# A second layer with seven products in place of eight, and casts and transposes that take strict turns

## The chip, the cores and the metric

The kernel runs on one core of a Trainium2 chip. The metric is the device time of one execution in microseconds (us). The profile gives the *span*, from the first to the last instruction; a timed execution is some 1.7 to 2.3 us longer than its span (401.6 for a span of 399.7, 428.7 for 426.6). A run is called slow when it is over 1.5% above the fastest of the same kernel, and only fast runs are compared.

## The reference

```python
# x, f_logit: (4, 6144, 256) float32; lower_bound: (256,)
sig = 1 / (1 + exp(-f_logit))
f = lower_bound + (1 - lower_bound) * sig
for t in range(6144):                      # a recurrence along the sequence
    h = f[:, t] * h + (1 - f[:, t]) * x[:, t]
    y[:, t] = h
y = y.reshape(24576, 256)
out = maximum(y @ w1, y @ w2) @ w_out      # w1, w2: (256, 1024); w_out: (1024, 256)
```

## The kernel before

The tokens come in *blocks* of 512, 48 of them, and two blocks make a *chunk* of 1024 (the first four blocks are chunks of their own, so chunks 4 to 25 hold two blocks each: 22 chunks, 21 periods between them). The kernel uses max(a, b) = a + relu(b - a): the *first layer* gives relu(y (w2 - w1)), and the *second layer* adds y (w1 w_out) to relu(...) w_out. So a block needs 16 first-layer products with 512 columns and 40 second-layer products with 256 columns.

The recurrence wants channels on partitions, and the inputs lie the other way round. From chunk 4 on, each input goes through three steps: a *cast* (a DMA on GpSimd's queue, float32 to bf16, into a scratch in memory), a *transpose* (a DMA on SyncE's queue, scratch to the tile fT or xT), and then the *gate* (a sigmoid on ScalarE), decay, drive and scan on VectorE. Each tensor has two scratches. A cast waits only until the transpose that last read its scratch has landed.

```python
    def fetch(c):
        b, t0, nt, _ = chunks[c]
        for s in range(2):
            src = srcs[s][b, t0 : t0 + nt, :]
            if by_xbar(c, s):
                scr = scratch[s][uses[s] % NSCR]
                uses[s] += 1
                nc.gpsimd.dma_start(
                    out=scr[0:nt, :].rearrange("(p i) d -> p (i d)", p=P),
                    in_=src.rearrange("(p i) d -> p (i d)", p=P),
                )
                held[c, s] = scr
            else:
                nat = natpool.tile([P, CH // P, D], BF16, name=("fn", "xn")[s])
                nc.gpsimd.dma_start(
                    out=nat[:, 0 : nt // P, :].rearrange(
                        "p (k i) d -> p k (i d)", i=TB // P
                    ),
                    in_=src.rearrange(
                        "(k p i) d -> p k (i d)", p=P, i=TB // P
                    ),
                )
                held[c, s] = nat
# ... cut ...
    def cross(c):
        nt = chunks[c][2]
        for s in range(2):
            if by_xbar(c, s):
                dst = inpool.tile([P, KC, CH], BF16, name=("fT", "xT")[s])
                nc.sync.dma_start_transpose(
                    out=dst[:, :, 0:nt], in_=held[c, s][0:nt, :]
                )
                held[c, s] = dst
# ... cut ...
    def gate(j):
        nb = blocks[j][2]
        u = midpool.tile([P, KC, TB], BF16, name="u")
        fT = turned[j, 0]
        nc.scalar.activation(
            out=like(u[:, :, 0:nb], fT), in_=fT, func=AF.Sigmoid, scale=-1.0
        )
        us[j] = u
# ... cut ...
    def first_layer(j, fc):
        nb = blocks[j][2]
        y = ys[j]
        dT = ps_d.tile([P, TB], FP32, name="dT")
        for kc in range(KC):
            nc.tensor.matmul(
                dT[:, 0:nb],
                lhsT=wd[:, kc, fc * P : (fc + 1) * P],
                rhs=y[:, kc, 0:nb],
                start=(kc == 0),
                stop=(kc == KC - 1),
            )
        rt = rpool.tile([P, TB], BF16, name="rt")
        nc.scalar.activation(out=rt[:, 0:nb], in_=dT[:, 0:nb], func=AF.Relu)
        rts[j, fc] = rt
# ... cut ...
            left = y[:, s, i:nb:ns] if s < KC else rts[j, s - KC][:, i:nb:ns]
            right = w13[:, s, :] if s < KC else wob[:, s - KC, :]
            nc.tensor.matmul(
                ps[:, r, :],
                lhsT=left,
                rhs=right,
                start=(s == 0 and (r == 0 or j == NBLK - 1)),
                stop=(s == n - 1 and (r == 1 or j == NBLK - 1)),
                skip_group_check=True,
            )
# ... cut ...
    LEAD_FETCH = 7
    LEAD_CROSS = 3
    done = {"fetch": 0, "cross": 0}

    def ahead(kind, fn, j):
        while done[kind] < NCHUNK and chunks[done[kind]][3] <= j:
            fn(done[kind])
            done[kind] += 1
# ... cut ...
        for j in range(2, NBLK + 1):
            ahead("cross", cross, j + LEAD_CROSS)
            ahead("fetch", fetch, j + LEAD_FETCH)
            steps = turn_steps(j + 2) if j + 2 < NBLK else []
            gates = {}
            if j + 1 < NBLK and by_xbar(blocks[j + 1][3], 0):
                gates[0] = j + 1
            if j + 2 < NBLK and not by_xbar(blocks[j + 2][3], 0):
                gates[FC // 2] = j + 2
            # ... cut ...
                if j < NBLK:
                    first_layer(j, fc)
                if j > 2:
                    second_layer(j - 1, fc)
                n = len(steps)
                turn(steps[fc * n // FC : (fc + 1) * n // FC])
                if fc in gates:
                    gate(gates[fc])
                if fc == 0 and 2 < j < NBLK - 1:
                    scans = scan_steps(j + 1)
                if fc < len(scans):
                    scans[fc]()
```

In block j the loop does the gate of block j+1, the scan of block j+1, the first layer of block j and the second layer of block j-1.

Of the kernel before, what the change touches and what calls it, by code (L numbers as in the profile page):

```python
# [18 lines left out]
def kernel(  # L19
# [18 lines left out]
    CH = 1024  # L38
    assert S % CH == 0

# [15 lines left out]
    def by_xbar(c, s):  # L56
        return c >= 4
# [6 lines left out]
    natpool = ctx.enter_context(tc.tile_pool(name="nat", bufs=6))  # L64
    inpool = ctx.enter_context(tc.tile_pool(name="inp", bufs=5))
    midpool = ctx.enter_context(tc.tile_pool(name="mid", bufs=2))
    ypool = ctx.enter_context(tc.tile_pool(name="ypool", bufs=4))
    rpool = ctx.enter_context(tc.tile_pool(name="rpool", bufs=2 * FC + 4))
    opool = ctx.enter_context(tc.tile_pool(name="opool", bufs=4))
    ps_t = ctx.enter_context(  # L70
        tc.tile_pool(name="ps_t", bufs=2, space=bass.MemoryType.PSUM)
    )
    ps_d = ctx.enter_context(
        tc.tile_pool(name="ps_d", bufs=3, space=bass.MemoryType.PSUM)
    )
    ps_o = ctx.enter_context(
        tc.tile_pool(name="ps_o", bufs=3, space=bass.MemoryType.PSUM)
    )

    NSCR = 2  # L80
    scratch = [
        [dram.tile([CH, D], BF16, name=f"scr{s}_{q}") for q in range(NSCR)]
        for s in range(2)
    ]
    uses = [0, 0]
# [5 lines left out]
    def fetch(c):  # L91
        b, t0, nt, _ = chunks[c]
        for s in range(2):
            src = srcs[s][b, t0 : t0 + nt, :]
            if by_xbar(c, s):
                scr = scratch[s][uses[s] % NSCR]
                uses[s] += 1
                nc.gpsimd.dma_start(  # L98
                    out=scr[0:nt, :].rearrange("(p i) d -> p (i d)", p=P),
                    in_=src.rearrange("(p i) d -> p (i d)", p=P),  # L100
                )
                held[c, s] = scr
            else:
                nat = natpool.tile([P, CH // P, D], BF16, name=("fn", "xn")[s])
                nc.gpsimd.dma_start(
                    out=nat[:, 0 : nt // P, :].rearrange(
                        "p (k i) d -> p k (i d)", i=TB // P
                    ),
                    in_=src.rearrange(
                        "(k p i) d -> p k (i d)", p=P, i=TB // P  # L110
                    ),
                )
                held[c, s] = nat
# [3 lines left out]
    def fetch_first(k):  # L117
        nt = TB // 2
        for s in range(2):
            raw = const.tile([P, nt // P, D], FP32, name=f"raw{k}{s}")  # L120
            nc.sync.dma_start(  # L121
                out=raw[:],
                in_=srcs[s][0, k * nt : (k + 1) * nt, :].rearrange(
                    "(p i) d -> p i d", p=P
                ),
            )
            raws[k, s] = raw

    def first_bf16(k, s, copy):
        raw = raws[k, s]  # L130
        nat = const.tile([P, raw.shape[1], D], BF16, name=f"nat{k}{s}")
        copy(out=nat[:], in_=raw[:])
        raws[k, s] = nat

    def first_turn(k):
        nt = TB // 2
        for s in range(2):
            dst = ps_t.tile([P, KC, nt // P, P], BF16, name="tT")
# [9 lines left out]
    def cross(c):  # L148
        nt = chunks[c][2]
        for s in range(2):  # L150
            if by_xbar(c, s):
                dst = inpool.tile([P, KC, CH], BF16, name=("fT", "xT")[s])
                nc.sync.dma_start_transpose(  # L153
                    out=dst[:, :, 0:nt], in_=held[c, s][0:nt, :]
                )
                held[c, s] = dst

    def turn_steps(j):
        b, t0, nb, c, o = blocks[j]
        steps = []  # L160
        for s in range(2):
            if by_xbar(c, s):
                turned[j, s] = held[c, s][:, :, o : o + nb]
                continue
            dst = ps_t.tile([P, KC, TB], BF16, name="tT")
            ns = nb // P
            turned[j, s] = dst[:, :, 0:nb].rearrange("p k (i m) -> p k m i", i=ns)
            for q in range(ns):
                for h in range(KC):
                    steps.append(  # L170
                        (
                            dst[:, h, q * P : (q + 1) * P],
                            held[c, s][:, o // P + q, h * P : (h + 1) * P],
                        )
                    )
# [7 lines left out]

    us = {}

    def gate(j):
        nb = blocks[j][2]
        u = midpool.tile([P, KC, TB], BF16, name="u")
        fT = turned[j, 0]
        nc.scalar.activation(  # L190
            out=like(u[:, :, 0:nb], fT), in_=fT, func=AF.Sigmoid, scale=-1.0
        )
        us[j] = u
# [6 lines left out]
    def scan_steps(j):  # L200
        b, t0, nb, c, o = blocks[j]
        u = us[j]
        ff = midpool.tile([P, KC, TB], BF16, name="ff")
        v = midpool.tile([P, KC, TB], BF16, name="v")
        y = ypool.tile([P, KC, TB], BF16, name="y")
        ys[j] = y

        def decay(h):
            nc.vector.tensor_scalar(  # L209
                out=ff[:, h, 0:nb],  # L210
                in0=u[:, h, 0:nb],
                scalar1=nom[:, h : h + 1],
                scalar2=1.0,
                op0=ALU.mult,
                op1=ALU.add,
            )

        def drive():
            xT = turned[j, 1]
            nc.vector.tensor_tensor(  # L220
                out=like(v[:, :, 0:nb], xT),
                in0=like(u[:, :, 0:nb], xT),
                in1=xT,
                op=ALU.mult,
            )

        def scan(h):
            if t0 == 0:
                init = 0.0
            else:  # L230
                pn = blocks[j - 1][2]
                init = ys[j - 1][:, h, pn - 1 : pn]
            nc.vector.tensor_tensor_scan(  # L233
                out=y[:, h, 0:nb],
                data0=ff[:, h, 0:nb],
                data1=v[:, h, 0:nb],
                initial=init,
                op0=ALU.mult,
                op1=ALU.add,
            )  # L240

        return [
            lambda: decay(0),
            lambda: decay(1),
            drive,
            lambda: scan(0),
            lambda: scan(1),
        ]

    first = {}  # L250

    def first_recurrence(k):
        nt = TB // 2
        cols = slice(k * nt, (k + 1) * nt)
        if k == 0:
            for t in ("u", "ff", "v"):
                first[t] = midpool.tile([P, KC, TB], BF16, name=t)
            ys[0] = ypool.tile([P, KC, TB], BF16, name="y")
        u, ff, v, y = (*(first[t] for t in ("u", "ff", "v")), ys[0])
        fT, xT = raws[k, 0], raws[k, 1]  # L260
        nc.scalar.activation(
            out=like(u[:, :, cols], fT), in_=fT, func=AF.Sigmoid, scale=-1.0
        )
        for h in range(KC):
# [7 lines left out]
            )  # L272
        nc.vector.tensor_tensor(
            out=like(v[:, :, cols], xT), in0=like(u[:, :, cols], xT), in1=xT,
            op=ALU.mult,
        )
        for h in range(KC):
# [13 lines left out]

    ident_f = const.tile([P, P], FP32)
# [8 lines left out]
    wdf = wpool.tile([P, KC, DFF], FP32)  # L301
    wd = wpool.tile([P, KC, DFF], BF16)
    w1T = wpool.tile([P, FC, D], BF16)
    w13 = wpool.tile([P, KC, D], BF16)
    NG = 2
    NQ = FC // NG
    w1n = [wpool.tile([P, KC, NQ * P], FP32, name=f"w1n{g}") for g in range(NG)]
    w2n = [wpool.tile([P, KC, NQ * P], FP32, name=f"w2n{g}") for g in range(NG)]

    def half(w, g):  # L310
        return w[g][:].rearrange("p kc (m q) -> p kc q m", q=NQ)

    def fcs(w, kc, g):
        return w[:, kc, g * NQ * P : (g + 1) * NQ * P].rearrange(
            "p (q m) -> p q m", q=NQ
        )
# [12 lines left out]
    def make_wd(fc, n):  # L329
        g, r = divmod(fc, NQ)  # L330
        qs = slice(r, r + n)
        cols = slice(fc * P, (fc + n) * P)
        nc.vector.tensor_tensor(  # L333
            out=wdf[:, :, cols].rearrange("p kc (q m) -> p kc q m", q=n),
# [4 lines left out]
        for kc in range(KC):  # L339
            if g == 0:  # L340
                nc.scalar.mul(wd[:, kc, cols], wdf[:, kc, cols], om[:, kc : kc + 1])  # L341
            else:
                nc.vector.tensor_scalar_mul(
                    out=wd[:, kc, cols], in0=wdf[:, kc, cols], scalar1=om[:, kc : kc + 1]
                )

    def turn_w1(k):
        g, r = divmod(k, NQ // 2)
        pt = ps_o.tile([P, KC, 2, P], FP32, name="psO")
# [11 lines left out]
    def make_w13():  # L361
        for kc in range(KC):
            psw = ps_o.tile([P, 2, D], FP32, name="psO")
# [9 lines left out]

    rts = {}

    def first_layer(j, fc):
        nb = blocks[j][2]
        y = ys[j]
        dT = ps_d.tile([P, TB], FP32, name="dT")
        for kc in range(KC):  # L380
            nc.tensor.matmul(  # L381
                dT[:, 0:nb],
                lhsT=wd[:, kc, fc * P : (fc + 1) * P],
                rhs=y[:, kc, 0:nb],
# [3 lines left out]
        rt = rpool.tile([P, TB], BF16, name="rt")  # L388
        nc.scalar.activation(out=rt[:, 0:nb], in_=dT[:, 0:nb], func=AF.Relu)  # L389
        rts[j, fc] = rt  # L390
# [3 lines left out]
    def second_layer(j, slot):  # L394
        b, t0, nb, c, o = blocks[j]
        ns = nb // P
# [3 lines left out]
        for k in range(slot * total // FC, (slot + 1) * total // FC):  # L400
            i, s = divmod(k, n)
            g, r = divmod(i, 2)
            if s == 0 and (r == 0 or j == NBLK - 1):
                acc["ps"] = ps_o.tile([P, 2, D], FP32, name="psO")
# [3 lines left out]
            left = y[:, s, i:nb:ns] if s < KC else rts[j, s - KC][:, i:nb:ns]  # L408
            right = w13[:, s, :] if s < KC else wob[:, s - KC, :]
# [8 lines left out]
            if j == NBLK - 1 and s == n - 1:  # L418
# [3 lines left out]
                r0 = b * S + t0  # L422
                (nc.sync if r else nc.scalar).dma_start(
# [148 lines left out]
```

## Time and profile before

The three runs took 438.17, 401.23 and 438.83 us. It has a fast and a slow state. The profile is of the slow one.

| | kernel before, slow profile |
|---|---|
| span | 428.3 us |
| TensorE / ScalarE / VectorE busy | 92% / 63% / 58% |
| transposes, issue to landing (medians) | 15 to 16 us for fT, 9 for xT |
| chunk period (issue of transposes to the next) | 11 to 23 us, mean 17.0 |

The page of the kernel before gives the span, the chain of work that ended last (share of the span by engine, then by line) and, per group, busy time, mean ns of one, then idle time before the group and what ended it:

```profile
span 428.3 us, 6970 instructions
...
PE 46%; DMA 34%; SPq 15%; ACT 3%; DVE 1%; issue 1%; ACTq 0%
PE psO L410 25%; DMA fT<-scr_0_90 20%; PE dT L381 19%; SPq L153 13%; DMA fT<-scr_1_91 12%; ACT u L190 2%; DMA w1n_110<-in_moe_w_dram 2%; SPq L433 1%; PE psO L352 1%; ACT rt L389 1%; PE tT L180 1%; PE psO L365 0%; SPq L121 0%; DVE osb L430 0%; DVE y L233 0%
...
L389 ACT ACTIVATE rt<-dT 128x512 bf16<-128x512 f32 x384 | 219.2, 598 | 104.1 <-PE dT L381 100.0
L381 PE MATMUL dT<-y,wd 128*128 128x512 bf16 x720 | 219.5, 384 | 21.3 <-ACT rt L389 19.5
L410 PE MATMUL psO<-wob,rt 128*128 128x256 bf16 x1536 | 230.7, 274 | 2.7 <-issue 0.4
...
L190 ACT ACTIVATE u<-fT 128x1024 bf16<-128x1024 bf16 x44 | 46.4, 1054 | 35.5 <-DMA fT<-scr_1_91 18.2
```

A third of the chain is transposing DMAs, with the issue queue of SyncE (SPq L153) on top: in this state TensorE is not alone in setting the time. The view of waits of the same kernel (engine, tile, line <- what it waited for: us in total, times, longest):

```profile
POOL scr_0_90 L98 <- DMA fT<-scr_0_90: 149.7, 10, 17.7
...
PE dT L381 <- ACT rt L389: 19.5, 11, 4.0
ACT u L190 <- DMA fT<-scr_1_91: 18.2, 7, 4.6
ACT u L190 <- DMA fT<-scr_0_90: 17.3, 8, 5.2
```

The gate waits for fT, relus queue behind the gate, and TensorE waits for relus. A stretch of the timeline without stalls (start, duration, engine, line, operation) shows the pace of TensorE:

```profile
203.69 0.60 PE L381 MATMUL dT<-y,wd 128*128 128x512 bf16 x2
...
204.12 0.38 PE L410 MATMUL psO<-w_109,y 128*128 128x256 bf16 x2
...
204.34 0.49 PE L410 MATMUL psO<-wob,rt 128*128 128x256 bf16 x3
...
204.67 0.59 PE L381 MATMUL dT<-y,wd 128*128 128x512 bf16 x2
```

One slot (two first-layer and five second-layer products) takes 204.67 - 203.69 = 0.98 us. Eight slots make a block, 7.82 us, and a pair of blocks takes 15.64 us.

### The profile page before, as it was taken

To read this page: it belongs to the slowest core of one execution; us is meant where nothing else is said; L and a number is where in the kernel's file an instruction comes from. 1 tells how busy PE (TensorE), PEld (TensorE's weight loads), DVE (VectorE), ACT (ScalarE), POOL (GpSimd) and SP (SyncE) were. 2 spreads that over 40 slices of the span, in tenths; PEclk is the share of its full clock that TensorE was granted. 3 is DMA by queue.
4 is the path that set the end of the run, shared out by engine and by line. 5 is a ranking of instruction groups with operands and counts; after the bars stand their busy time and mean duration, and the time that the engine had idled before them with its cause. 6 is when DMAs were issued, how large, how long until landed. Compare 5 with 4: busy or idle time off the path is not lost.

```text
span 428.3 us, 6970 instructions
## 1 busy us (share of the span) xinstructions
PE 392.8 (92%) x2744; PEld 296.8 (69%) x2792; DVE 248.7 (58%) x359; ACT 268.5 (63%) x447; POOL 26.4 (6%) x58
## 2 busy tenths in 40 slices
PE   3999979798789999998997899999998999999996
PEld 1677756576557777776775577767676777777775
DVE  5785637455357566564653557657547656567551
ACT  3656656557366676675673666756657676776762
POOL 1400000000000000000000000000000000000000
PEclk9999999999989999999999699999999999999999
DMA  7999999999999999999998999999999999998112
GB/s 245 222 220 198 123 157 141 137 169 252 81 240 226 119 239 233 112 248 168 183 237 75 218 158 186 250 145 170 219 131 231 226 216 164 268 157 179 79 69 100
DMA packets 103377, 77.01 MB, mean 180 GB/s; under 512 B 93552, under 2 KB 94064, under 8 KB 102640
## 3 DMA queue, kind: packets, MB, share of 16 engines
q1 hardware_dynamic: 100512, 51.13, 66.7%
q0 software_dynamic: 2544, 25.17, 36.1%
q8 instruction: 22, 0.36, 0.4%
q10 hardware_dynamic: 288, 0.26, 0.2%
q14 instruction: 11, 0.09, 0.1%
HBM read 53.48 MB, written 48.23 MB: 237 GB/s over the span
## 4 chain that ended last, share of the span: by engine, by line
PE 46%; DMA 34%; SPq 15%; ACT 3%; DVE 1%; issue 1%; ACTq 0%
PE psO L410 25%; DMA fT<-scr_0_90 20%; PE dT L381 19%; SPq L153 13%; DMA fT<-scr_1_91 12%; ACT u L190 2%; DMA w1n_110<-in_moe_w_dram 2%; SPq L433 1%; PE psO L352 1%; ACT rt L389 1%; PE tT L180 1%; PE psO L365 0%; SPq L121 0%; DVE osb L430 0%; DVE y L233 0%
## 5 line engine op out<-in xcount | busy, mean ns | idle before, releaser
L389 ACT ACTIVATE rt<-dT 128x512 bf16<-128x512 f32 x384 | 219.2, 598 | 104.1 <-PE dT L381 100.0
L381 PE MATMUL dT<-y,wd 128*128 128x512 bf16 x720 | 219.5, 384 | 21.3 <-ACT rt L389 19.5
L410 PE MATMUL psO<-wob,rt 128*128 128x256 bf16 x1536 | 230.7, 274 | 2.7 <-issue 0.4
L410 PEld LDWEIGHTS <-rt 128*128 128x128 bf16 x1536 | 170.7, 114 | 41.4 <-issue 1.1
L233 DVE TENSOR_TENSOR_SCAN y<-ff,y,v 128x512 bf16<-128x512 bf16 x88 | 107.9, 1268 | 0.1
L430 DVE COPY osb<-psO 128x512 f32<-128x512 f32 x94 | 64.7, 690 | 59.0 <-PE psO L410 58.9
L381 PEld LDWEIGHTS <-wd 128*128 128x128 bf16 x768 | 75.8, 99 | 33.2 <-issue 24.6
L209 DVE TENSOR_SCALAR ff<-u,nom 128x512 bf16<-128x512 bf16 x94 | 29.0, 351 | 105.0 <-ACT u L190 105.0
L410 PE MATMUL psO<-w_109,y 128*128 128x256 bf16 x384 | 74.0, 275 | 0.0
L410 PEld LDWEIGHTS <-y 128*128 128x128 bf16 x384 | 43.4, 113 | 42.6 <-issue 3.5
L190 ACT ACTIVATE u<-fT 128x1024 bf16<-128x1024 bf16 x44 | 46.4, 1054 | 35.5 <-DMA fT<-scr_1_91 18.2
L220 DVE TENSOR_TENSOR v<-u,xT 128x1024 bf16<-128x1024 bf16 x44 | 30.3, 688 | 3.8 <-DMA xT<-scr_0_92 1.8
L98 POOL DMA_DIRECT2D scr_0_90<-in_f_logit_dram x11 | 5.4, 493 | 149.7 <-DMA fT<-scr_0_90 149.7
L98 POOL DMA_DIRECT2D scr_1_91<-in_f_logit_dram x11 | 5.3, 486 | 148.8 <-DMA fT<-scr_1_91 148.1
L233 DVE TENSOR_TENSOR_SCAN y<-ff,v 128x512 bf16<-128x512 bf16 x6 | 7.0, 1208 | 0.0
L98 POOL DMA_DIRECT2D scr_0_92<-in_x_dram x11 | 5.4, 488 | 18.7 <-DMA xT<-scr_0_92 16.9
L98 POOL DMA_DIRECT2D scr_1_93<-in_x_dram x11 | 5.3, 486 | 15.7 <-DMA xT<-scr_1_93 14.9
L190 ACT ACTIVATE u<-tT 128x1024 bf16<-128x1024 bf16 x3 | 3.2, 1058 | 4.3 <-PE tT L180 4.3
L352 PE MATMUL psO<-ident_f,w1n_110 128*128 128x128 f32 x8 | 1.9, 422 | 3.4 <-DMA w1n_110<-in_moe_w_dram 3.4
L341 ACT ACTIVATE wd<-wdf,om 128x128 bf16<-128x128 f32 (+1 forms) x6 | 2.2, 428 | 4.3 <-DVE wdf L333 4.3
L352 PEld LDWEIGHTS psO<-ident_f,w1n_110 128*128 128x128 f32 x8 | 1.6, 221 | 3.7 <-issue 3.7
L220 DVE TENSOR_TENSOR v<-u,tT 128x1024 bf16<-128x1024 bf16 x3 | 3.6, 1216 | 0.0
(49 smaller groups left out, 45.1 us busy)
## 6 DMA issues: line engine op xcount, KB each, us to landing
out_dram<-osb SPq DMA_DIRECT2D x47, 512.0 KB, 4.8
scr_0_90<-in_f_logit_dram POOLq DMA_DIRECT2D x11, 512.0 KB, 7.5
scr_0_92<-in_x_dram POOLq DMA_DIRECT2D x11, 512.0 KB, 12.4
scr_1_91<-in_f_logit_dram POOLq DMA_DIRECT2D x11, 512.0 KB, 7.9
scr_1_93<-in_x_dram POOLq DMA_DIRECT2D x11, 512.0 KB, 13.6
fn<-in_f_logit_dram POOLq DMA_DIRECT2D x3, 256.0 KB, 7.9
xn<-in_x_dram POOLq DMA_DIRECT2D x3, 256.0 KB, 8.6
w2n_112<-in_moe_w_dram SPq DMA_DIRECT2D x1, 512.0 KB, 6.5
```

The lines of the kernel that those rows point to most:

```text
L98: nc.gpsimd.dma_start(out=scr[0:nt, :].rearrange("(p i) d -> p (i d)", p=P), in_=src.rearrange("(p i) d -> p (i d)", p=P),)
L153: nc.sync.dma_start_transpose(out=dst[:, :, 0:nt], in_=held[c, s][0:nt, :])
L180: nc.tensor.transpose(dst, src, ident[:])
L190: nc.scalar.activation(out=like(u[:, :, 0:nb], fT), in_=fT, func=AF.Sigmoid, scale=-1.0)
L209: nc.vector.tensor_scalar(out=ff[:, h, 0:nb], in0=u[:, h, 0:nb], scalar1=nom[:, h : h + 1], scalar2=1.0, op0=ALU.mult, op1=ALU.add,)
L220: nc.vector.tensor_tensor(out=like(v[:, :, 0:nb], xT), in0=like(u[:, :, 0:nb], xT), in1=xT, op=ALU.mult,)
L233: nc.vector.tensor_tensor_scan(out=y[:, h, 0:nb], data0=ff[:, h, 0:nb], data1=v[:, h, 0:nb], initial=init, op0=ALU.mult, op1=ALU.add,)
L352: nc.tensor.transpose(pt[:, kc, q, :], half(w1n, g)[:, kc, 2 * r + q], ident_f[:])
L381: nc.tensor.matmul(dT[:, 0:nb], lhsT=wd[:, kc, fc * P : (fc + 1) * P], rhs=y[:, kc, 0:nb], start=(kc == 0), stop=(kc == KC - 1),)
L389: nc.scalar.activation(out=rt[:, 0:nb], in_=dT[:, 0:nb], func=AF.Relu)
L410: nc.tensor.matmul(ps[:, r, :], lhsT=left, rhs=right, start=(s == 0 and (r == 0 or j == NBLK - 1)), stop=(s == n - 1 and (r == 1 or j == N ...
L430: nc.vector.tensor_copy(out=osb[:, 2 * g : 2 * g + 2, :], in_=ps[:])
```

## The change

The intent was twofold. First, fewer columns on TensorE: for three quarters of the hidden units (HC = 3 of each 4 groups of 128) the second layer of a *pair* of blocks is done as a 2x2 block product with seven products instead of eight (Winograd's form of Strassen's scheme). Rows are the two blocks, columns the two halves of the output, and the inner dimension the two halves of the units. VectorE forms four sums of relus per pair (sum1 to sum4), and partial results are held in PSUM banks and copied to SBUF (the snapshots). Second, steadier DMA: one scratch per tensor, and *strict turns*. The casts of chunk c+1 are issued only when both transposes of chunk c have landed, and the transposes of c+1 wait for both casts.

```diff
+    HC = 3
# ... cut ...
-    natpool = ctx.enter_context(tc.tile_pool(name="nat", bufs=6))
-    inpool = ctx.enter_context(tc.tile_pool(name="inp", bufs=5))
+    inpool = ctx.enter_context(tc.tile_pool(name="inp", bufs=4))
     midpool = ctx.enter_context(tc.tile_pool(name="mid", bufs=2))
-    ypool = ctx.enter_context(tc.tile_pool(name="ypool", bufs=4))
-    rpool = ctx.enter_context(tc.tile_pool(name="rpool", bufs=2 * FC + 4))
+    ypool = ctx.enter_context(tc.tile_pool(name="ypool", bufs=7))
+    rpool = ctx.enter_context(tc.tile_pool(name="rpool", bufs=10))
+    spool = ctx.enter_context(tc.tile_pool(name="spool", bufs=5))
+    snpool = ctx.enter_context(tc.tile_pool(name="snpool", bufs=5))
# ... cut ...
-    NSCR = 2
-    scratch = [
-        [dram.tile([CH, D], BF16, name=f"scr{s}_{q}") for q in range(NSCR)]
-        for s in range(2)
-    ]
-    uses = [0, 0]
+    scratch = [dram.tile([CH, D], BF16, name=f"scr{s}") for s in range(2)]
# ... cut: fetch takes one tensor at a time; scr = scratch[s] ...
     def cross(c):
-        nt = chunks[c][2]
-        for s in range(2):
-            if by_xbar(c, s):
-                dst = inpool.tile([P, KC, CH], BF16, name=("fT", "xT")[s])
-                nc.sync.dma_start_transpose(
-                    out=dst[:, :, 0:nt], in_=held[c, s][0:nt, :]
-                )
-                held[c, s] = dst
+
+        if c >= NCHUNK:
+            return
+        for s in (1, 0):
+            dst = inpool.tile([P, KC, CH], BF16, name=("fT", "xT")[s])
+            nc.sync.dma_start_transpose(out=dst[:], in_=scratch[s][:])
+            held[c, s] = dst
+        if c + 1 < NCHUNK:
+            for s in (1, 0):
+                pool_waits(held[c, s][:, 0, 0:1])
+            for s in range(2):
+                fetch(c + 1, s)
# ... cut: pair_gate, pair_scans (1024-wide u, ff, v in place of 512-wide) ...
+    def make_sevens():
+        b11, b12 = wob[:, 0:HC, lo], wob[:, 0:HC, hi]
+        b21, b22 = wob[:, KH : KH + HC, lo], wob[:, KH : KH + HC, hi]
+
+        def minus(out, a, b):
+            return lambda: nc.vector.tensor_tensor(
+                out=out, in0=a, in1=b, op=ALU.subtract
+            )
+
+        steps = [
+            minus(t1[:], b12, b11),
+            minus(t3[:], b22, b12),
+            minus(t2[:], b22, t1[:]),
+            minus(t4[:], b21, t2[:]),
+            minus(w13d[:], w13[:, :, lo], w13[:, :, hi]),
+        ]
+        if wcd is not None:
+            steps.append(minus(wcd[:], wob[:, :, lo], wob[:, :, hi]))
+        return steps
# ... cut ...
+        if fc % 2:
+            nc.scalar.activation(
+                out=rts[j, k][:, g - 1 : g + 1, :].rearrange(
+                    "p q (i m) -> p q i m", m=P
+                ),
+                in_=dT[:].rearrange("p q (m i) -> p q i m", m=P),
+                func=AF.Relu,
+            )
+
# ... cut ...
+    def sum3(p):
+        sum_of(p, 3, quarter(p, 0, 0), quarter(p, 1, 0), ALU.subtract)
+
+    def sum2(p):
+        sum_of(p, 2, quarter(p, 1, 1), sums[p, 3][:], ALU.subtract)
+
+    def sum1(p):
+        sum_of(p, 1, quarter(p, 1, 0), quarter(p, 1, 1), ALU.add)
+
+    def sum4(p):
+        sum_of(p, 4, quarter(p, 0, 1), sums[p, 2][:], ALU.subtract)
# ... cut ...
+        product("X", part(0, 0), lambda k: wob[:, k, lo], True)
+        then(snapshot("X", 1))
+        product("B", part(0, 1), lambda k: wob[:, KH + k, lo], True)
+        linear("B", ja, lo, False)
+        then(leave("B", ja, lo, 1, False))
+        product("X", sub(2), lambda k: t2[:, k, :])
+        then(snapshot("X", 2))
+        product("E", sub(1), lambda k: t1[:, k, :], True)
+        then(snapshot("E", 5))
+        product("X", sub(3), lambda k: t3[:, k, :])
+        linear("X", jb, hi, False)
+        then(leave("X", jb, hi, 5, False))
+        product("E", sub(4), lambda k: wob[:, KH + k, hi])
+        linear("E", ja, hi, False)
+        then(leave("E", ja, hi, 2, True))
+        product("X", part(1, 1), lambda k: t4[:, k, :])
+        linear("X", jb, lo, True)
+        then(leave("X", jb, lo, None, True))
# ... cut ...
+        for p in range(PAIR0, NPAIR):
+            first = p == PAIR0
+            more = p + 1 < NPAIR
+            seq = []
+            if more:
+                scans = pair_scans(p + 1)
+                seq += [
+                    (0, scans["decay"]),
+                    (10, scans["drive0"]),
+                    (40, scans["scan00"]),
+                    (52, scans["scan01"]),
+                    (76, scans["drive1"]),
+                    (84, scans["scan10"]),
+                    (104, scans["scan11"]),
+                    (124, lambda: sum3(p)),
+                ]
+            if not first:
+                seq += [
+                    (4, lambda: sum2(p - 1)),
+                    (20, lambda: sum1(p - 1)),
+                    (64, lambda: sum4(p - 1)),
+                ]
+            seq.sort(key=lambda e: e[0])
+            steps = [] if first else sevenths(p - 1)
+            done_steps = 0
+            gates = {5: 0, 11: 1, 13: 2, 15: 3} if p + 2 < NPAIR else {}
+            for slot in range(2 * FC):
+                first_layer(2 * p + slot // FC, slot % FC)
+                if first:
+                    if slot % 2 == 0:
+                        second_layer(2 * p - 1, slot // 2)
+                upto = (slot + 1) * len(steps) // (2 * FC)
+                for step in steps[done_steps:upto]:
+                    step()
+                done_steps = upto
+                while seq and seq[0][0] < (slot + 1) * 9:
+                    seq.pop(0)[1]()
+                if slot == 2 and p + 3 < NPAIR:
+                    cross(blocks[2 * p + 6][3])
+                if slot in gates:
+                    pair_gate(p + 2, gates[slot])
+        for j in (NBLK - 2, NBLK - 1):
+            for slot in range(FC):
+                second_layer(j, slot)
```

The loop of pair p does the first layer of p, the second layer of p-1, the scans of p+1, and the gates of p+2.

## The prediction

> **What bounds the kernel now.** Where nothing stalls, a slot (one pair of first-layer products, five second-layer products) takes 0.98 us in the timeline: 2 x 0.216 + 5 x 0.109. That is 7.82 us per 512-token block, 15.64 per pair, with TensorE back to back. But the chain of waits gives 34% to transposing DMAs (fT<-scr) and 13% to their issue queue. In the timeline TensorE's starts are late by 38 us in all after 34 us. Without those stalls the span of 428 would be 390. The timed runs (401 and twice 438) are about 10 us above these two numbers, so I read 401 as TensorE-bound and 438 as DMA-stalled. In the packet records a transposing packet takes 18 ns alone and 70 to 125 while a cast is in flight; chunk periods run from 14 to 20 us, mean 17.
>
> **TensorE, per pair of blocks.** Plain: 80 products of 256 columns (8.74 us). New: 7x4x3=84 plus 64 plain ones, 148 of 128 columns. The trace's 128-column transposes, each with its own weight load, start every 55.6 ns: 148 x 55.6 = 8.23 us. (The Trainium skill, "TensorE: Matmul & The Clock Gate", section Back-to-back issue gap, gives about 81 ns for streams with loads at 128 columns; that would be 12.0 us and a loss. I trust the trace.) The period becomes 15.14: 0.5 us x 21 pairs = 10 us gained.
>
> **Other engines, estimates from group means.** ScalarE: 8 wide relus of about 1.03 (two at 0.53), 4 gates and 4 copies of 0.6: 13.0 us per pair (was 11.7). VectorE: decays 1.2, drives 1.4, scans 4.9, three adds 2.1, four 1536-wide sums of about 1.0: 13.6 (was 10.3). Both fit in 15.1, with little room.
>
> **DMA decides.** Bytes are unchanged, but the turns become a closed loop: casts land, transposes, transposes land, casts. From the packets: two casts uncontended 5.0 us, two transposes 5.2; landing to issue 1.0 to 1.3 each; cast issue to data 2.1; transpose issue to data about 1.3. Sum: 15 to 16.5 us per chunk, with stores hidden in the gaps. (The skill, "DMA: Bandwidth & Descriptors", section Anatomy of one DMA, puts the fixed cost near 2 us; the trace agrees.) The first chunk lands at about 35 us, 21 periods follow, and the last needs some 50 us of work after it: 14.3 us would leave TensorE the bound (span about 385, time 395), 15.0 gives a time of 410, 16.0 gives 431. What speaks for the short end is that contention disappears and three chunks of lead absorb jitter. The bimodality should mostly vanish.
>
> **Prediction: 408 us, 8 in 10 between 388 and 438.** Faster by over 2%: 0.68; within 2%: 0.17; slower: 0.15.
>
> **Right or wrong in the profile.** TensorE: 128-column products start every 56 ns, slot about 0.945 us; otherwise the 55.6 is wrong. Relu 128x1024 about 1.03 us in spite of strided PSUM reads; sum about 1.0 us. Transposing packets stay near 18 ns; cast and transpose intervals do not overlap; the period between transposes tells which bound holds. If DMA binds, gates wait for fT and the chain names DMA and POOL; if not, TensorE has over 60% of the chain.
>
> **What would make it wrong.** Weight loads limiting 128-column products (each 10 ns costs 31 us over the kernel); turn latency above 16.5 us (no gain or loss); VectorE late with sums or bank releases, stalling TensorE; startup stalls, because chunk 5 is cast only after chunk 4 is transposed; a before that runs in its 401 state, against which the gain is small or none.

## The result

The changed kernel is correct and took 429.04 us (median of 4 runs, 425.64 to 430.86). A timed execution is some 1.7 to 2.3 us longer than its span (401.6 for a span of 399.7, 428.7 for 426.6). Against the fast runs of the kernel before in the same rounds the ratio is 1.069, interval 1.062 to 1.076: slower by 7%. A ratio is the mean time of one kernel's fast runs over that of the other's fast runs of the same rounds, so it is not quite the ratio of the medians quoted. The slow state of the kernel before is about as slow as the changed kernel.

The page of the changed kernel, with the lines that answer to those above. L427 is the relu, now 1024 wide; L597 is the seven-product layer, L488 the sums, L268 the gate:

```profile
span 426.6 us, 9672 instructions
...
DMA 60%; PE 20%; SPq 10%; POOL 4%; issue 3%; DVE 2%; ACT 2%; POOLq 0%; ACTq 0%
DMA scr<-in_x_dram 34%; DMA fT<-scr 24%; SPq L145 9%; PE dT L419 8%; PE ps L466 6%; PE ps L597 5%; POOL scr L94 2%; POOL waited L332 2%; ACT r L427 1%; DMA osb<-in_x_dram 1%; DVE r L339 1%; PE ps L172 1%; PE ps L373 0%; SPq L112 0%; DVE w1T L367 0%
...
L419 PE MATMUL dT<-y,wd 128*128 128x512 bf16 x696 | 213.2, 385 | 32.6 <-ACT r L427 30.4
L427 ACT ACTIVATE r<-dT 128x1024 bf16<-128x1024 f32 x192 | 194.1, 1023 | 69.6 <-PE dT L419 69.3
...
L597 PE MATMUL ps<-wob,r 128*128 128x128 bf16 x1008 | 108.2, 219 | 0.7
...
L268 ACT ACTIVATE u<-fT 128x512 bf16<-128x512 bf16 x88 | 55.0, 629 | 45.1 <-DMA fT<-scr 42.7
...
L488 DVE TENSOR_TENSOR S<-r 128x1536 bf16<-128x1536 bf16 x42 | 40.0, 951 | 4.3 <-ACT r L427 4.3
```

TensorE's share of the chain fell from 46% to 20%. Casts (scr<-in_x_dram) and transposes (fT<-scr) hold 58%. The view of waits of the changed kernel:

```profile
POOL waited L332 <- DMA xT<-scr: 264.8, 21, 16.1
...
ACT u L268 <- DMA fT<-scr: 42.7, 20, 7.0
...
POOL waited L332 <- DMA fT<-scr: 34.5, 21, 3.3
PE dT L419 <- ACT r L427: 30.4, 20, 5.2
```

The same path as before: gate behind fT (42.7 us in all), TensorE behind relu (30.4 us). The chain of the changed kernel in order of time, two turns of it:

```profile
194.82 9.54 DMA scr<-in_x_dram
204.41 2.01 SPq L145
206.52 5.92 DMA fT<-scr
212.56 0.18 POOL waited L332
...
213.01 0.48 POOL scr L94
213.49 7.59 DMA scr<-in_x_dram
221.12 3.06 SPq L145
```

This is a closed loop: cast of x, issue of the transposes, transpose of f, the wait of the casting queue, the next cast. From 204.41 to 221.12 it takes 16.71 us. And in the timeline of the changed kernel at the same place:

```profile
212.53 0.63 ACT L268 ACTIVATE u<-fT 128x512 bf16<-128x512 bf16 x1 [4.30 <-DMA fT<-scr]
...
213.53 1.94 ACT L427 ACTIVATE r<-dT 128x1024 bf16<-128x1024 f32 x2
...
214.60 0.59 PE L419 MATMUL dT<-y,wd 128*128 128x512 bf16 x2 [3.62 <-ACT r L427]
```

ScalarE had stood idle for 4.30 us when fT landed and the gate began; two relus followed it in ScalarE's order; TensorE had then stood idle for 3.62 us.

From the packet records, the mean turn of the changed kernel divides as follows (21 turns):

| step of one turn | mean us | predicted |
|---|---|---|
| transposes: issue to first data | 1.31 | 1.3 |
| transposes: data, both | 5.10 | 5.2 |
| landing and waits, to issue of the casts | 1.25 | 1.0 to 1.3 |
| casts: issue to first data | 1.37 | 2.1 |
| casts: data, both | 6.40 | 5.0 |
| landing, to issue of the next transposes | 0.76 | 1.0 to 1.3 |
| sum | 16.19 | 15 to 16.5 |

### The profile page after: what moved, and what is told of

Same layout as the page of the kernel before. It is cut to its first block, busy times and chain, and to the rows that moved or that the text cites. A ratio compares the mean times of both kernels' runs of the same rounds, so it can differ in the third digit from the quotient of the medians.

```text
span 426.6 us, 9672 instructions
## 1 busy us (share of the span) xinstructions
PE 381.6 (89%) x4148; PEld 284.0 (67%) x4220; DVE 302.8 (71%) x384; ACT 288.4 (68%) x383; POOL 47.4 (11%) x100
## 4 chain that ended last, share of the span: by engine, by line
DMA 60%; PE 20%; SPq 10%; POOL 4%; issue 3%; DVE 2%; ACT 2%; POOLq 0%; ACTq 0%
DMA scr<-in_x_dram 34%; DMA fT<-scr 24%; SPq L145 9%; PE dT L419 8%; PE ps L466 6%; PE ps L597 5%; POOL scr L94 2%; POOL waited L332 2%; ACT r L427 1%; DMA osb<-in_x_dram 1%; DVE r L339 1%; PE ps L172 1%; PE ps L373 0%; SPq L112 0%; DVE w1T L367 0%
## 5 line engine op out<-in xcount | busy, mean ns | idle before, releaser
L419 PE MATMUL dT<-y,wd 128*128 128x512 bf16 x696 | 213.2, 385 | 32.6 <-ACT r L427 30.4
L427 ACT ACTIVATE r<-dT 128x1024 bf16<-128x1024 f32 x192 | 194.1, 1023 | 69.6 <-PE dT L419 69.3
L597 PEld LDWEIGHTS <-r 128*128 128x128 bf16 x1428 | 106.2, 98 | 39.3
L597 PE MATMUL ps<-wob,r 128*128 128x128 bf16 x1008 | 108.2, 219 | 0.7
L597 PEld LDWEIGHTS <-S 128*128 128x128 bf16 x1008 | 67.7, 98 | 29.8
L268 ACT ACTIVATE u<-fT 128x512 bf16<-128x512 bf16 x88 | 55.0, 629 | 45.1 <-DMA fT<-scr 42.7
L555 DVE TENSOR_TENSOR osb<-ps,sn 128x512 f32<-128x512 f32 x63 | 43.5, 690 | 41.5 <-ACT sn L543 16.5
L597 PE MATMUL ps<-w,y 128*128 128x128 bf16 x504 | 66.2, 219 | 0.2
L597 PEld LDWEIGHTS <-y 128*128 128x128 bf16 x672 | 58.0, 113 | 9.9
L597 PE MATMUL ps<-t,S 128*128 128x128 bf16 x756 | 59.3, 219 | 0.5
L488 DVE TENSOR_TENSOR S<-r 128x1536 bf16<-128x1536 bf16 x42 | 40.0, 951 | 4.3 <-ACT r L427 4.3
L488 DVE TENSOR_TENSOR S<-r,S 128x1536 bf16<-128x1536 bf16 x42 | 39.6, 944 | 1.7 <-ACT r L427 1.7
L466 PE MATMUL ps<-wob,r 128*128 128x256 bf16 x192 | 27.8, 283 | 0.1
L466 PEld LDWEIGHTS <-r 128*128 128x128 bf16 x192 | 19.4, 101 | 4.6 <-issue 0.6
L597 PE MATMUL ps<-t,r 128*128 128x128 bf16 x252 | 20.9, 219 | 0.2
L597 PE MATMUL ps<-wob,S 128*128 128x128 bf16 x252 | 20.9, 219 | 0.2
```

The costliest lines, as they stand in the source:

```text
L268: nc.scalar.activation(out=mids[p + NBLK, "u"][:, h, cols], in_=held[c, 0][:, h, cols], func=AF.Sigmoid, scale=-1.0,)
L419: nc.tensor.matmul(dT[:, fc % 2, :], lhsT=wd[:, kc, fc * P : (fc + 1) * P], rhs=y[:, kc, :], start=(kc == 0), stop=(kc == KC - 1),)
L427: nc.scalar.activation(out=rts[j, k][:, g - 1 : g + 1, :].rearrange("p q (i m) -> p q i m", m=P), in_=dT[:].rearrange("p q (m i) -> p q i ...
L466: nc.tensor.matmul(ps[:, r, :], lhsT=left, rhs=right, start=(s == 0 and (r == 0 or j == NBLK - 1)), stop=(s == n - 1 and (r == 1 or j == N ...
L488: nc.vector.tensor_tensor(out=t[:], in0=a, in1=b, op=op)
L555: nc.vector.tensor_tensor(out=dst, in0=bank[b][:], in1=snap[name][:], op=ALU.add)
```

## Experiments

Three explanations were compared. **Theory L**: the closed loop of turns sets the time. **Rival E**: VectorE and ScalarE, busier now, stall TensorE with their in-order queues. **Rival P**: the pipeline of pairs loses time at start and end. The first round forced a sharper version of L, called **theory D** below. All kernels gave correct results except the one that is wrong.

### 1. The changed kernel with the DMA scheme of before

```diff
-    scratch = [dram.tile([CH, D], BF16, name=f"scr{s}") for s in range(2)]
+    scratch = [[dram.tile([CH, D], BF16, ...) for q in range(2)] for s in range(2)]
-        for s in (1, 0):                       # transposes: x, f
+        for s in range(2):                     # f, x, from scratch[s][c % 2]
-            for s in (1, 0):
-                pool_waits(held[c, s][:, 0, 0:1])
-                fetch(c + 1, s)
+                fetch(c + 2, s)
# ... cut: chunks 1 to 5, not 1 to 4, are fetched ahead of the loop ...
```

> The changed kernel with the DMA scheme of before: two scratches per tensor, no strict turns, f before x, casts of chunk c+2 issued as soon as the transposes of chunk c release the scratch. Theory L (the closed loop cast, land, transpose, land of 16.2 us per chunk sets the time, the seven-product layer itself is a gain): the loop is broken, so the time falls clearly below 429; with TensorE stalls gone it would be about 379 (426.6 span less 49.7 us of late TensorE starts, plus 2), with chunk periods of 14 to 17 under contention 380 to 415, perhaps in two states. Rival E (VectorE and ScalarE, now near full, with their in-order queues make the loss): stays at 425 to 432. Rival P (the pipeline of pairs loses at start and end): stays within 1% of 429.

Measured: 440.47 us median (439.43 to 444.77), ratio 1.101. That is slower still, and theory L had expected a clear fall. Its waits:

```profile
ACT u L269 <- DMA fT<-scr: 46.6, 13, 9.2
...
PE dT L420 <- ACT r L428: 36.3, 13, 7.4
```

The gate still waits for fT. In this profile 21,454 of 90,112 transposing packets began while cast data was in flight, and took 68 ns on average; the others took 26. (The median is 18 ns in both groups. The difference is made by few packets: 4% of those that met casts took over 100 ns, 1.2 us each on average, against 0.8% of the others. The prediction's 18 against 70 to 125 sets a typical packet against means.) Without turns the two kinds of transfer collide. So L was not refuted, but this way of opening the loop brought back what strict turns remove.

### 2. The kernel before with strict turns

```diff
-                scr = scratch[s][uses[s] % NSCR]
+                scr = scratch[s]
-        for s in range(2):   # transposes
+        for s in (1, 0):
+        if c + 1 < NCHUNK:
+            for s in (1, 0):
+                pool_waits(held[c, s][:, 0, 0:1])
+            fetch(c + 1)
-    LEAD_CROSS = 3
+    LEAD_CROSS = 5
```

> The kernel before with only the DMA part of the change: one scratch per tensor, x transposed before f, the queue that casts waits for both transposes; transposes are issued up to five blocks ahead. Theory L: the loop of about 16.2 us per chunk now rules here too, against 15.64 of TensorE: 28 + 21 x 16.2 + about 38 us of work after the last chunk gives a span near 406 to 415, slower than the fast state of before (401), without its second state. Rivals E and P: the DMA part costs nothing or helps; 392 to 401.

Measured: 400.80 us median (400.36 to 401.70), ratio 1.0004. The turns cost nothing here, against L's 406 to 415 of span. Yet its period is 15.97 us, longer than TensorE's 15.64. Its page:

```profile
span 399.3 us, 7085 instructions
...
PE 65%; DMA 24%; SPq 4%; DVE 3%; issue 1%; POOL 1%; ACT 1%; POOLq 0%; ACTq 0%
```

So nearly the same loop of turns is harmless in one kernel and costs 7% in the other. Two things differ: TensorE needs a chunk every 15.17 us there and every 15.64 here, and a chunk is needed earlier there. The second leads to theory D: *the span is the time at which the last chunk's gate can start, plus the work that must follow that gate*, unless TensorE's own work is longer. The last chunk's first gate, in the timelines of ScalarE, is at 370.34 us in the strict before,

```profile
370.34 1.06 ACT L189 ACTIVATE u<-fT 128x1024 bf16<-128x1024 bf16 x1 [1.55 <-DMA fT<-scr]
```

and at 375.81 us in the changed kernel:

```profile
375.81 0.63 ACT L268 ACTIVATE u<-fT 128x512 bf16<-128x512 bf16 x1 [3.04 <-DMA fT<-scr]
```

These differ by only 5.5 us. But 399.3 - 370.3 = 28.9 us follow in the first and 426.6 - 375.8 = 50.8 us in the second. The gates of pair p+2 stand in the loop of pair p, from slot 5 of 16. Behind the last gate come the rest of that loop, two whole loops of 15.17 us and the plain second layer of two blocks.

### 3. The changed kernel with almost no casts

```diff
-        if c + 1 < NCHUNK:
+        if c + 1 < 6:
```

> The changed kernel with the casts of chunks 6 and later left out (their transposes read stale scratch, so the result is wrong on purpose; transposes, stores and all compute stay). Theory L: TensorE-bound, a span of 377 to 382 and a time of 379 to 384; the pair takes 14.9 to 15.0 us. Rival E: the engines still stall, 415 or more. Rival P: about 400 to 415.

The result is wrong (stale scratch). Measured: 398.83 us median (397.94 to 401.12), ratio 0.995. The period of a pair is exactly 15.17 us from pair 4 on, so the engines keep up: rival E falls. But the time is 399 and not 380. Two things explain it. My 379 was wrong: I had summed late starts of TensorE in the changed kernel's trace, and 72 matmul records are missing from that trace (4148 of 4220), so gaps in the records were counted as stalls. And at the start TensorE waits twice, 3.3 and 3.7 us, behind gates that wait for fT of chunks 4 and 5 (chunk 5 is cast only after chunk 4 has been transposed). These gates have no other wait for fT in the whole run:

```profile
ACT u L268 <- DMA fT<-scr: 10.7, 2, 5.5
```

Rival P has a part: about 7 us at the start.

### 4. The kernel before again

No edit: it was run again for a profile of the fast state.

> The kernel before, unchanged, for a profile in its other state if chance gives it. If 401 is the TensorE-bound state, the span is 399, late TensorE starts after 34 us sum to about 8 us (427 less 390 was 38 in the recorded profile), and the chunk period of the transposes is at most 15.7 us with fewer transposing packets above 50 ns.

Measured: 401.20 us, and this profile fell in the fast state:

```profile
span 399.7 us, 7018 instructions
...
PE 96%; DMA 2%; SPq 1%; issue 0%; DVE 0%
```

Every pair takes 15.64 us and TensorE is never late. The expected 8 us of late starts are not there: they were the missing records again (2744 of 2792 in the slow profile, all 2792 in this one). So TensorE's bound for the kernel before is about 399 (spans of 399.7 here, 399.3 in experiment 2 and 399.1 in experiment 8), not 390. In the slow profile 23,350 transposing packets began during cast data (mean 70 ns), in the fast one 1,954, in the strict one none.

### 5. The strict before, with gates two blocks earlier

```diff
-            if j + 1 < NBLK and by_xbar(blocks[j + 1][3], 0):
-                gates[0] = j + 1
+            if 2 < j and j + 3 < NBLK:
+                turn_steps(j + 3)
+                gates[0] = j + 3
# ... cut: at j = 2 the gates of blocks 4 and 5 are computed first ...
-    LEAD_CROSS = 5
+    LEAD_CROSS = 7      # and five buffers for u
```

> The kernel before with strict turns (which ran at 400.8, spans 399), and one thing more: each gate is computed two blocks earlier, so a chunk is needed 15.6 us before it was, as the changed kernel does with its pipeline of pairs. Theory D (the time is the landing of the last chunk plus the work that must follow it: about 370 + 29 in the strict before, 375 + 51 in the changed kernel): the span rises by about 15 us to 412 to 417. If the lead of a gate does not matter (rival E: the loss lies in the seven-product engines), it stays at 399 to 401.

Measured: 414.28 us (412.71 to 416.95), ratio 1.033. The last chunk's gate starts where it did,

```profile
370.60 1.06 ACT L190 ACTIVATE u<-fT 128x1024 bf16<-128x1024 bf16 x1 [1.42 <-DMA fT<-scr]
```

and the span of the profile is 415.2: 44.6 us follow instead of 28.9. No seven products are in this kernel, only the earlier need, and the 15.7 us that theory D expected are lost. They are lost at the start, where ScalarE waits for the first chunks and TensorE for ScalarE:

```profile
54.64 1.06 ACT L190 ACTIVATE u<-fT 128x1024 bf16<-128x1024 bf16 x1 [7.40 <-DMA fT<-scr]
...
56.23 1.01 PE L381 MATMUL dT<-y,wd 128*128 128x512 bf16 x2 [6.20 <-ACT rt L389]
```

The first layer of block 4 begins at 61.9 us, in experiment 2 at 46.3; from there to block 46 both take 15.7 us a pair. So this run shows what an earlier need costs. It does not show that the cost depends on slow turns (see the sum below).

### 6. The changed kernel with a delay in each turn

```diff
+            nc.gpsimd.memset(idle[:], 0.0)      # 128x2048, between waits and casts
             for s in range(2):
                 fetch(c + 1, s)
```

> The changed kernel with one idle clearing of a 128x2048 tile on the queue that issues the casts, between the waits and the casts of each turn (some 2 us, to be read from its trace as d). Theory L/D (the loop of turns paces everything): the time rises by 21 x d, about 42 us for 2 us, to 465 to 475. Rival E: the DMA has slack, rises by less than 10 us.

Measured: 450.11 us (446.40 to 451.28), ratio 1.122. The delay, from the groups of GpSimd (busy time, mean ns):

```profile
L150 POOL MEMSET idle<- 128x2048 f32 x21 | 37.9, 1805 | 0.0
```

With d = 1.8 us, 21 x d would be 38 us. The span rose by 448.1 - 426.6 = 21.5 us, and the last gate came 21.0 us later (396.8). So the loop is closed, since a delay in it lengthens the program, but it is not stiff: the period rose by 1.10 us and not by 1.8, so the time rose by half of what theory L had expected. In the records the wait to the casts' issue grew by 1.58, while the casts' data shrank from 6.40 to 6.13 and their start lag from 1.37 to 1.19. A store's packets met those of a chunk's casts in 7 of 22 chunks of the changed kernel and in 2 here. That explains a part at most: the casts that met none took 6.23 and 6.05 us on average. The rest stays open.

### 7. Turns kept apart, but the loop opened

```diff
+    scratch: two per tensor, as in experiment 1
+        if c > 5 and c + 1 < NCHUNK:
+            nc.sync.dma_start(out=peek[:], in_=scratch[0][(c + 1) % 2][0:1, 0:16])
         # transposes of c: f, x
-                pool_waits(held[c, s][:, 0, 0:1])
-                fetch(c + 1, s)
+                fetch(c + 2, s)
```

The read of 32 bytes holds SyncE's queue until the f cast of the next chunk has landed. It orders transposes behind casts without depending on the data that they read. It does not wait for the x cast, so the two are not wholly apart: 3,593 transposing packets still began during cast data (39 ns on average), a third of them those of chunks 4 and 5, which have no read before them.

> The changed kernel with the turns kept apart but the loop opened: two scratches per tensor, f before x, casts of chunk c+2 issued when the transposes of c release the scratch, and from chunk 6 on a 32-byte read of the newly cast f scratch ahead of the transposes of c+1, so that they start when that cast has landed and not while it runs. Theory L/D: the two waiting times for landing overlap with data, the period falls from 16.2 to 13.5 to 15.2 us, TensorE binds: a span of 389 to 397, time 391 to 399, and ACT no longer waits for fT after the first pairs. Rival E: stays above 415.

Measured: 401.65 us (400.75 to 405.33), ratio 1.004, not distinguishable from the fast before and 27 us below the changed kernel. The pair takes 15.17 us from pair 4 to the end, and the transposes run ahead (14.3 us per chunk). The waits for fT fell from 42.7 us in the changed kernel to 11.2, all of it before 75 us:

```profile
ACT u L271 <- DMA fT<-scr: 11.2, 4, 6.3
```

The time is above the expected 391 to 399, again because of the start: the first layer of block 6 begins at 67.3 us, where about 59 was possible by the pace of the slots.

### 8. The kernel before with the same opened turns

```diff
+        (the same 32-byte read; casts of c + 2 issued in cross; LEAD_CROSS = 5)
```

> The kernel before with the same opened, kept-apart turns. TensorE-bound at 7.82 us a block in every run: 400 to 402, and none of the runs at 430 to 450 that the kernel before shows.

Measured: 401.21 us (400.45 to 401.77), ratio 1.001, no slow run, as expected. Experiments 2 and 8 had no slow run in 8, where the kernel before had 10 in 32. With a chance of 10 in 32, eight fast runs in a row would come by luck in 5% of cases.

### 9. The changed kernel, strict turns kept, with later gates

```diff
-            gates = {5: 0, 11: 1, 13: 2, 15: 3} if p + 2 < NPAIR else {}
+            gates = {0: (0, 1), 1: (2,), 2: (3,)} if more else {}
-                    pair_gate(p + 2, gates[slot])
+                    pair_gate(p + 1, q)
-                    (0, scans["decay"]),
-                    (10, scans["drive0"]),
+                    (30, scans["decay"]),
+                    (34, scans["drive0"]),
# ... cut: the same move ahead of the loop, and where the tile u is made ...
```

> The changed kernel, strict turns kept, with the gates of a pair moved from slots 5, 11, 13, 15 of the loop two pairs ahead to slots 0, 0, 1, 2 of the loop one pair ahead (decay and first drive follow at slot 3): each chunk is needed 10 us later. Theory D (landing of the last chunk plus the work behind it): the span falls by about 10 us to 414 to 418, time 416 to 420, with the period of the turns still near 16.2 us. If the lead does not matter: 426 to 431.

Measured: 418.20 us (median of the three fast runs, 413.99 to 418.71; a fourth took 420.89 and counts as slow), ratio 1.039, where the changed kernel has 1.069. The period of the turns is 16.21 us, as before. The last gate,

```profile
374.52 1.15 ACT L268 ACTIVATE u<-fT 128x512 bf16<-128x512 bf16 x2
```

and a span of 416.4: 41.9 us follow instead of 50.8. It came out as theory D said.

### 10. Opened turns and late gates together

```diff
+        (the edit of experiment 7: second scratch, 32-byte read, casts of c + 2)
-            gates = {5: 0, 11: 1, 13: 2, 15: 3} if p + 2 < NPAIR else {}
+            gates = {0: (0, 1), 1: (2,), 2: (3,)} if more else {}      # pair p + 1, as in 9
# ... cut: the other lines of experiment 9 ...
```

> Opened, kept-apart turns and late gates together. Pair period 15.17 us as in the opened version; its remaining loss was at the start (block 6 began at 67.3 us where 59.1 was possible, about 8 us of late starts). With late gates I expect block 6 at 59 to 63 us and a span of 390 to 395, time 392 to 397: 1 to 2.2% faster than the fast state of before. If VectorE cannot fit the later decays the pair period rises above 15.3 us.

Measured over five rounds: 396.16 us (394.71 to 398.60), ratio 0.989, interval 0.986 to 0.992. It beats the changed kernel by 33 us and the fast state of the kernel before by 1.1%, which is clear of the noise but small, with no slow run in 6. Block 6 begins at 59.9 us, as expected. Its page:

```profile
span 393.1 us, 9649 instructions
...
PE 82%; DMA 12%; ACT 2%; issue 1%; POOL 1%; SPq 1%; DVE 0%; ACTq 0%
```

### 11. The same, with the guard one chunk later

```diff
-        if c > 5 and c + 1 < NCHUNK:
+        if c > 6 and c + 1 < NCHUNK:
```

> The same, with the guard that keeps transposes and casts apart beginning one chunk later, so that the transposes of chunk 6 are not held back at the start. Expect within 3 us of the former; better if the start is still held by chunk 6.

Measured: 393.76 to 410.26 us, three of six runs in a slow state; the fast runs give 0.991. With the transposes of chunk 6 left free beside casts, nothing is gained that could be told from noise. Three slow runs of six against none of six are too few to show that this edit makes the kernel unsteady.

### 12. One scratch, no strict waits

```diff
-            for s in (1, 0):
-                pool_waits(held[c, s][:, 0, 0:1])
-            for s in range(2):
+            for s in (1, 0):
                 fetch(c + 1, s)
```

> The changed kernel with one scratch per tensor kept, and only the strictness removed: no waits of the casting queue for both transposes; x is cast as soon as its own scratch is free, then f. Each tensor goes round its own loop. Theory L: landing times of one tensor overlap with data of the other, the period falls under 15.2 to 15.5 us and the time to 399 to 405 as with the opened turns; if contention of casts and transposes takes it back, the period is 16 to 17 and the time 425 to 440, as with two scratches and no guard (440).

Measured: 406.66, 407.26, 424.03 and 525.98 us. The fast runs give 1.015, with a pair period of 15.17 us after a slow start (pair 4 waits; block 8 begins at 88.9 us). So half of the expectation held: letting one tensor's landing overlap the other's data does shorten the loop, to 14.7 us per chunk. But the runs are unsteady, and what made one of them 526 us was not looked into.

### The sum of theory D

| kernel | turn period, us | last chunk's first gate | work behind it | span |
|---|---|---|---|---|
| before, strict turns | 15.97 | 370.3 | 28.9 | 399.3 |
| before, strict, gates two blocks earlier | 15.86 | 370.6 | 44.6 | 415.2 |
| changed | 16.19 | 375.8 | 50.8 | 426.6 |
| changed, late gates | 16.21 | 374.5 | 41.9 | 416.4 |
| changed, delay in each turn | 17.28 | 396.8 | 51.3 | 448.1 |

The work behind the gate was read as span less gate, so the rows add up by construction. What the runs test is that the last gate hardly moves when only the need is moved (370.3 and 370.6; 375.8 and 374.5) and moves by 21.0 us when the turns are delayed, and that the work behind is what the loops contain: for the changed kernel 11 of 16 slots, two loops and the last second layer, by the pace 10.4 + 30.3 + 8.7 = 49.5 us, measured 50.8.

Theory D does not say when the time is lost. The starts of the first layer's weight loads, none of which is missing, do:

| kernel | block 6 begins | mean pair, block 6 to 46 |
|---|---|---|
| before, strict turns | 62.0 | 15.69 |
| before, strict, gates two blocks earlier | 77.6 | 15.70 |
| changed | 71.1 | 16.38 |
| changed, late gates | 59.8 | 16.44 |
| changed, opened turns (7) | 67.3 | 15.18 |
| changed, opened turns, late gates (10) | 59.9 | 15.25 |

The early need is paid at the start, with strict turns (71.1 less 59.8, 11.3 us) and with opened ones (7.4 us). The rate of the turns is paid pair by pair: 20 pairs at 16.38 in place of 15.18 are 24 us. The start has a part that was not tried apart: TensorE's granted clock is recorded as half from 49.0 to 55.9 and from 66.1 to 69.5 us in the changed kernel, around its stalls there, and nowhere before the end in experiment 10; 10 us at half clock are at most 5 us of work.

## Why the prediction was wrong

- **Pace of TensorE: right.** The 128-column products start every 56 ns (201.797, 201.853, 201.909 us and on in the trace), the pair takes 15.17 us (15.14 predicted), and 21 x (15.64 - 15.17) = 9.9 us of TensorE time were saved. The Trainium skill's figure of about 81 ns ("TensorE: Matmul & The Clock Gate", section Back-to-back issue gap) does not fit this stream; the measurement decides.
- **ScalarE and VectorE: right.** The relu of 1024 took 1023 ns (1.03 predicted) with strided PSUM reads, the sums 944 to 951 ns (1.0). Where chunks came in time (experiments 3, 7, 10) the pair held 15.17 us, so neither engine set the time.
- **The loop: right in mechanism and size.** 16.19 us in a predicted 15 to 16.5; the first gate at 34.3 us (35 predicted), and 50.8 us behind the last gate (50). Two terms were mis-sized in opposite directions, the casts' start lag (1.37 for 2.1) and the casts' data (6.40 for 5.0). That the sum still fits is in part luck. Why the casts' data took longer is open; the stores lie in the gaps, as predicted (11 of 6,016 store packets began during cast data).
- **The step that failed: "What speaks for the short end is that contention disappears and three chunks of lead absorb jitter."** Contention did disappear (no transposing packet during cast data, median 18 ns). But a slower mean rate uses a lead up: 21 turns of 16.19 us against 15.17 are 21.4 us. And there was no lead to use: the gate of the second transposed chunk already waits 7.05 us for fT, until 49.5 us. (In experiment 2 the 21 turns are only 6.9 us too slow in sum, and the lead lasts almost to the end.) The text's own line, 16.0 us giving 431, was within 2 us of the result, and the forecast of 408 and "faster" left it.
- **A second failed step: "Without those stalls the span of 428 would be 390" and timed runs "about 10 us above".** The bound is about 399 and a timed run 1.7 to 2.3 us above its span. Missing matmul records were read as stalls. So the 401 state was already free of stalls, and the hoped-for gain was 10 us from there and not 20 or 30 from the slow state.
- **What the prediction had as a constant** (some 50 us of work after the last chunk) was a part of the change. In the kernel before the same figure is 29. Those 22 us are most of the 27.3 us between the changed kernel and the strict before; the last gate's 5.5 us are the rest. By the time at which they are lost, 9 of the 27 us fall before block 6, 14 come from the pace of the pairs up to block 46, and 4 from the end.

Where the expected gain went: the 9.9 us of TensorE time are real, but off the path. In the changed kernel the path is 27.8 us to the first transpose issue, 21 turns of 16.19, about 8 us to the last gate, and 50.8 behind it: 27.8 + 339.9 + 8.1 + 50.8 = 426.6.

Still open: why the kernel before falls into its slow state in a third of its runs. The profiles show that the states differ in how many transposing packets meet casts, and keeping turns apart went with fast runs alone in experiments 2 and 8; what tips it was not tried. Nor was it tried to mend the rest of the start in experiment 10.

## What to carry to other kernels

Before a producer is made to take strict turns, add up one turn with its landing times, and compare it with the consumer's *mean* period: lead hides jitter, and a slower rate only until the lead is used up. A deeper software pipeline needs its first inputs earlier, and here that was paid at the start even with the faster producer (7.4 us between experiments 7 and 10); with the slower producer the turns' rate came on top. So ask of each stage how early its first input must arrive, and how much work must follow the last. To keep two kinds of transfer apart, order them without a data dependency (a second buffer and a small ordering read), so that one side's landing overlaps the other side's data.

## What the Trainium skill lacked or had wrong

- "TensorE: Matmul & The Clock Gate", section Back-to-back issue gap, gives about 81 ns per product for a stream of weight load and product at 128 columns. Here such a stream, each product with its own load, ran at 56 ns.
- "DMA: Bandwidth & Descriptors", section Rules for kernel authors, says that a DMA transpose next to ordinary DMAs "needs nothing". The results were right, but the cost in time is not told: transposing packets took 64 to 70 ns on average while casts were in flight, against 23 apart from them (kernel before, both profiles); the median was 18 ns in either case, and 4% of the packets made the difference. The same page's Issuing engines are not separate DMA queues, which says that DMAs of all issuing engines run on the same 16 engines and interleave, agrees with this.
- The same page's Two DMAs through the same engine are not ordered has the issuer wait for the first DMA's completion, as the strict turns do. It gives no figure for what such hand-overs cost in a turn; here 1.31 + 1.25 + 1.37 + 0.76 = 4.7 us of 16.2. Its fixed cost of about 2 us per DMA (Anatomy of one DMA, for DMAs that GpSimd issues) fits the casts' share, 1.37 + 0.76 = 2.1 us. The transposes, which SyncE issues, have 1.31 + 1.25 = 2.6.
- "Perfetto Trace Analysis" does not warn that gaps in TensorE's record may be missing records and not stalls: 48 of 2792 and 72 of 4220 were missing; the 48 were worth about 9 us in my reading (390 for 399).
